# Two units through the first MLP together: the second unit's attention moved beside the first's, its p turned by TensorE in float32

## The chip, the cores and the metric

The kernel runs on one core of a Trainium2 chip. The time is device microseconds from the first to the last instruction, the median of three runs: 1043.31 us before (1042.61 to 1045.53). TensorE (PE, weight loads PEld), VectorE (DVE), ScalarE (ACT), GpSimd (POOL) and the DMA queue of SyncE (SP) work side by side, each in its own fixed order of instructions, and wait for one another by semaphores.

## The reference

Inputs are q, k, v of 4 batches x 8 heads x 576 positions x 64 and a forget gate f (4 x 8 x 576). The weights of both MLPs arrive as float64 bit patterns, which the kernel itself turns into float32.

```python
scores = q @ k.T / 8 + cum[i] - cum[j]     # cum: cumulative sum of log(clip(f)); causal
x  = softmax(scores) @ v                   # 2304 tokens x 512 (8 heads x 64)
h  = x @ w_in                              # first MLP, 512 -> 2048
x1 = (s * relu(h)**2 + b) @ w_out          # 2048 -> 512
h2 = x1 @ w2_in                            # second MLP
out = leaky_relu(h2, 0.01) @ w2_out
```

## The kernel before

**Units.** The 2304 tokens are cut into nine units of 256 tokens. Units 0 to 3 are the first 256 positions of the four batches ("light": a head has 3 blocks of 128x128 scores), units 4 to 7 the next 256 positions and the last 64 ("heavy"), and unit 8 collects the four 64-token tails for the MLP. The first MLP runs unit by unit, 16 steps (`i`) each: `mlp1_h` (L700) makes 128 rows of h for 256 tokens, `mlp1_g` (L714) squares, `mlp1_o` (L740) adds into the output.

**Precision.** A float32 product is made of three passes in the fast float32r form: each operand is split into a high and a low part, and high x high, high x low and low x high are summed. Such a step takes 12 matmuls for h (4 blocks x 3) and 12 for o. The weights are made by `float_w` (L96: one ACT and three DVE instructions on 512 columns) and split by `split_w` (L108: an ACT copy and a POOL subtraction). There are 32 blocks of the first MLP's weights. For unit 0 the w_out blocks are not split: `mlp1_o` uses plain float32 matmuls there (L746, two instructions each in the profile), and the 16 w_out blocks are split during unit 1 (`split_late_to`).

**Attention.** Unit 0 has its own path, done in a startup loop (L622) before the first MLP: `first_a` makes scores, maximum and exponential of a head, `first_b` scales the probabilities p on POOL, turns them by three PE transposes (L597) and copies them out, `first_c` multiplies by v in float32 (L608) and splits the result into `xs[0]`. All other units go by slots, one tile (a head's rows) each, in three stages: `st_score` (L311), `st_split` (L354: p is split into two float16 halves by ACT and DVE and turned by a DMA transpose, L375), `st_av` (L377, AV matmuls L393 on a v that is split and turned in the same way). A pair of heads gathers in `x_raw` and is then split into `xs[u]` (`split_x1`, L426).

**Order.** `slots_to` emits slots beside the MLP steps, as `slot_target` (L668) says: during unit u's MLP the attention of unit u+1. The framework's scheduler then fixes each engine's order ahead of time from these priorities (`ahead`) and from its own estimate of when inputs are ready, so work whose inputs are there fills the gaps, as far as buffers allow: `x` has 2 buffers (units u and u+2 share one), `x_raw` 2, `p_t` and `p_hl` 3, `tt` 4. PSUM's eight banks before: `ps_o` 2 (outputs of two d in one bank), `ps_h` 2, `ps_s` 2, `ps_v` 2.

```python
for u in range(NU):                # L841
    slots_to(ends[u])
    for i in range(NF):            # L851
        ...
        ps = mlp1_h(u, i)
        g = mlp1_g(u, i, ps)
        slots_to(slot_target(u, i))
        if pending is not None: ... mlp1_o(pu, pi, pg, po)
```

Of the kernel before, what the change touches and what calls it, by code (L numbers as in the profile page):

```python
# [17 lines left out]
P = 128  # L18
# [20 lines left out]
def attention_moe_moe_kernel(  # L39
# [31 lines left out]
    wp = ctx.enter_context(tc.tile_pool(name="wp", bufs=2 * NF + 1))  # L71
    ps_o = ctx.enter_context(tc.tile_pool(name="ps_o", bufs=1, space=bass.MemoryType.PSUM))
    ps_h = ctx.enter_context(tc.tile_pool(name="ps_h", bufs=2, space=bass.MemoryType.PSUM))
# [4 lines left out]

    W_FLOAT = 0

# [13 lines left out]
    def float_w(raw, out=None):  # L96
# [7 lines left out]
        out = top if out else x  # L104
        nc.vector.scalar_tensor_tensor(out, low, 29, x, ALU.logical_shift_right, ALU.bitwise_or)  # L105
        return out.bitcast(F32)
# [7 lines left out]
    class Weights:  # L114


        def __init__(self, w_in, w_out, late):
            self.src = (w_in, w_out)
            self.late = late
            self.blocks, self.done, self.split = [], 0, late  # L120
# [4 lines left out]
        def split_to(self, n):  # L125
            while self.done < min(n, len(self.blocks)):
                n0 = self.done
                late = n0 % 2 == 1 and n0 // 2 >= self.late
                x = float_w(self.blocks[n0], late)
                self.blocks[n0] = x if late else split_w(x)  # L130
                self.done += 1

        def split_late_to(self, n):
            while self.split < min(n, NF):
                k = 2 * self.split + 1
                self.blocks[k] = split_w(self.blocks[k])
                self.split += 1
# [4 lines left out]

    w1, w2 = Weights(w_in1, w_out1, W_FLOAT), Weights(w_in2, w_out2, NF)

# [9 lines left out]
    mp = mlp1.enter_context(tc.tile_pool(name="mp", bufs=2, side="right"))  # L154
    att = ExitStack()
# [49 lines left out]
    def load_v(p):  # L205
        if p >= NP:
            return
        u, h = heads[2 * p]
        b, u0, un, _ = units[u]
        kend = u0 + un  # L210
        v_raw[2 * p] = wp.tile([P, 2 * DM], F32, tag="w", name="v_raw")
        nc.sync.dma_start(
            out=v_raw[2 * p][:, :kend], in_=vT[b, h : h + 2, :, :kend].rearrange("h d s -> (h d) s")
        )
# [16 lines left out]
    def split_pair_v(p):  # L231
        if p < NP:
# [121 lines left out]
    def st_split(i):  # L354
# [3 lines left out]
        tt, sm = t_t.pop(i), sm_t.pop(i)  # L358
        nc.vector.tensor_scalar(sm[:, 4 : 4 + nt], sm[:, 2 : 2 + nt], 1.0e-9, 1.0 / PSCALE, ALU.add, ALU.mult)
# [17 lines left out]
    def st_av(i):  # L377
        jb, n, ts, last = tiles[i]
        u, h, j, half = jobs[jb]
        b, u0, un, _ = units[u]  # L380
        if half or (n == 0 and h % 2 == 0):
            av_t[j // 2] = ps_a.tile([P, 512], F32, tag="ps_v", name="ps_v", bufs=2)
# [21 lines left out]
        if not half and h % 2 == 0:  # L404
            x_raw[u] = xp.tile([P, UN + NL], F32, tag="x_raw", name="x_raw", bufs=2)
        xr = x_raw[u]
        at = UN if half else 0
        for e in range(2) if half else [h % 2]:
            own, oth = slice(e * D, (e + 1) * D), slice((1 - e) * D, (2 - e) * D)
            m = NL if half else UN  # L410
            src, o = av[:, e * m : (e + 1) * m], xr[own, at : at + m]
# [4 lines left out]
        if pr == 0:  # L416
            xs[u] = xp.tile([P, 2, ND, UN], F32R, tag="x", name="x", bufs=2)
        inv = v_inv[j - j % 2][:, 4:5]
        with ahead(P_X):
            split_x1(xs[u], pr, xr[:, :UN], inv)  # L420
            if un > UN:
                xl = xr[:, UN:]
                nc.gpsimd.tensor_scalar(xl, xl, inv, 0.0, ALU.mult, ALU.add)
                nc.sync.dma_start(out=xld[pr * P : (pr + 1) * P, b * NL : (b + 1) * NL], in_=xl)

# [4 lines left out]
    def last_x1():  # L430
# [3 lines left out]
        x = xs[NU - 1] = xp.tile([P, 2, ND, UN], F32R, tag="x", name="x", bufs=2)  # L434
# [7 lines left out]
    P_RUN = 4000  # L442

# [6 lines left out]
    W_LATE = 6  # L450
# [38 lines left out]
    for r in range(ND // 2):  # L489
# [3 lines left out]
        if r == 0:  # L493
# [3 lines left out]
            nc.sync.dma_start(out=v_0, in_=v0.rearrange("(k p) c -> p k c", p=P))  # L497
# [4 lines left out]

    cl = wp.tile([P, 2 * DM], F32R, tag="w", name="cum_hl")
# [43 lines left out]
    xs[0] = xp.tile([P, 2, ND, UN], F32R, tag="x", name="x", bufs=2)  # L547
# [416 lines left out]
```

## Time and profile before

| | us |
|---|---|
| median of three runs | 1043.31 |
| profiled execution: its own time / span | 1039.49 / 1037.7 |
| startup, until the first MLP matmul of unit 0 | 0 to 43.6 |
| unit 0's MLP, first output copy | 129.5 |
| unit 1's MLP, first output copy | 191.8 |
| unit 2's MLP, first output copy | 261.4 |
| last output copy of the first MLP on ACT | 639.4 |

In a row of the view by stretches, the first numbers are the stretch and its length, then come each engine's busy time with its count of instructions, the granted TensorE clock as a share of full speed, the share of the DMA engines' time, and the GB/s they moved. In a timeline or chain row stand the start, the duration, and what ran; several like instructions are merged (x12). A matmul's duration includes its way through the array, so a busy PE is not yet a full PE: the distance between starts says how dense it is.

### The profile page before, as it was taken

To read this page: it belongs to the slowest core of one execution; us is meant where nothing else is said; L and a number is where in the kernel's file an instruction comes from. 1 tells how busy PE (TensorE), PEld (TensorE's weight loads), DVE (VectorE), ACT (ScalarE), POOL (GpSimd) and SP (SyncE) were. 2 spreads that over 40 slices of the span, in tenths; PEclk is the share of its full clock that TensorE was granted. 3 is DMA by queue.
4 is the path that set the end of the run, shared out by engine and by line. 5 is a ranking of instruction groups with operands and counts; after the bars stand their busy time and mean duration, and the time that the engine had idled before them with its cause. 6 is when DMAs were issued, how large, how long until landed. Compare 5 with 4: busy or idle time off the path is not lost.

```text
span 1037.7 us, 18127 instructions
## 1 busy us (share of the span) xinstructions
PE 986.1 (95%) x6664; PEld 851.0 (82%) x6664; DVE 537.9 (52%) x1410; ACT 521.3 (50%) x1283; POOL 151.8 (15%) x234
## 2 busy tenths in 40 slices
PE   7887789989999999999999999999999999999998
PEld 4676679879888888888999998778888888888897
DVE  6899773665667766777531399873111311211111
ACT  4777696655656766677643566552221221221232
POOL 4434424110101010100000135430000000000000
PEclk9899999999999999999999999999999999999999
DMA  8499491566889999989620463701000100100010
GB/s 282 152 245 269 89 211 40 136 134 134 186 155 181 180 179 197 185 170 192 90 83 2 168 239 94 239 13 49 33 1 1 61 1 1 41 0 1 1 41 21
DMA packets 184296, 116.68 MB, mean 112 GB/s; under 512 B 137040, under 2 KB 163152, under 8 KB 184208
## 3 DMA queue, kind: packets, MB, share of 16 engines
q1 hardware_dynamic: 184208, 115.53, 47.0%
q8 instruction: 52, 0.85, 0.3%
q14 instruction: 36, 0.29, 0.1%
HBM read 74.00 MB, written 10.04 MB: 81 GB/s over the span
## 4 chain that ended last, share of the span: by engine, by line
PE 47%; issue 3%; DVE 3%; POOL 2%; DMA 1%; ACT 1%; POOLq 0%; SPq 0%; ACTq 0%; DVEq 0%
PE ps_o L823 17%; PE ps_h L807 16%; PE ps_o L749 6%; PE ps_h L705 6%; POOL w L111 2%; PE ps_v L393 1%; DVE wt L103 1%; DMA w_raw<-in_moe_w_out 1%; DVE wt L105 1%; DVE wt L102 1%; PE ps_s L296 1%; DMA p_t<-p_hl 0%; ACT wt L101 0%; PE ps_s L283 0%; DVE g L730 0%
## 5 line engine op out<-in xcount | busy, mean ns | idle before, releaser
L705 PE MATMUL ps_h<-x,w 128*128 128x256 f32 x1728 | 242.9, 286 | 5.0 <-POOL w L111 3.3
L749 PE MATMUL ps_o<-g,w 128*128 128x256 f32 (+1 forms) x1536 | 226.8, 289 | 10.8 <-ACT g L729 6.3
L705 PEld LDWEIGHTS ps_h<-x,w 128*128 128x128 f32 x1728 | 220.4, 190 | 7.7 <-POOL w L111 3.9
L823 PE MATMUL ps_o<-w,g 128*128 128x512 f32 x864 | 216.1, 396 | 1.8 <-DVE g L815 1.8
L807 PE MATMUL ps_h<-x,w 128*128 128x512 f32 (+1 forms) x960 | 213.6, 370 | 0.0
L749 PEld LDWEIGHTS ps_o<-g,w 128*128 128x128 f32 x1536 | 197.3, 190 | 17.5 <-ACT g L729 7.9
L807 PEld LDWEIGHTS ps_h<-x,w 128*128 128x128 f32 x960 | 169.0, 188 | 34.4
L823 PEld LDWEIGHTS ps_o<-w,g 128*128 128x128 f32 x864 | 160.5, 188 | 41.5 <-DVE g L815 3.5
L815 DVE TENSOR_TENSOR g<-ps_h,g 128x512 fp32r<-128x512 f32 (+1 forms) x80 | 51.0, 637 | 258.3 <-ACT g L814 258.1
L813 ACT ACTIVATE ps_h<-ps_h 128x512 f32<-128x512 f32 (+1 forms) x80 | 43.1, 539 | 250.7 <-PE ps_h L807 250.7
L345 ACT ACTIVATE tt<-tt,sm 128x512 f32<-128x512 f32 (+4 forms) x128 | 76.0, 594 | 46.5 <-DVE sm L327 45.2
L371 DVE SCALAR_TENSOR_TENSOR p_hl<-tt,sm,p_hl 128x512 f16<-128x512 f32 (+4 forms) x128 | 77.5, 619 | 34.3 <-ACT p_hl L370 33.8
L370 ACT ACTIVATE p_hl<-tt,sm 128x512 f16<-128x512 f32 (+4 forms) x128 | 73.2, 595 | 40.2 <-DMA p_t<-p_hl 31.6
L111 POOL TENSOR_TENSOR w<-wt,w 128x512 fp32r<-128x512 f32 x48 | 73.6, 1537 | 98.0 <-ACT w L110 92.2
L730 DVE TENSOR_TENSOR g<-ps_h,g 128x256 fp32r<-128x256 f32 x128 | 53.6, 421 | 60.9 <-ACT g L729 59.6
L393 PE MATMUL ps_v<-p_t,v_st 128*128 128x128 f16 (+1 forms) x912 | 59.7, 211 | 14.7 <-DMA p_t<-p_hl 11.9
L727 ACT ACTIVATE ps_h<-ps_h 128x256 f32<-128x256 f32 x128 | 46.8, 367 | 50.3 <-PE ps_h L705 49.4
L393 PEld LDWEIGHTS <-v_st 128*128 128x128 f16 x912 | 44.3, 98 | 21.4 <-issue 13.2
L327 DVE CUSTOM_DVE_ANT_0 tt<-ps_s,cumk 128x512 f32<-128x512 f32 (+4 forms) x128 | 59.6, 497 | 2.2 <-PE ps_s L287 0.7
L101 ACT ACTIVATE wt<-w_raw 128x512 f32<-128x512 f32 x64 | 42.7, 672 | 28.2 <-POOL w L111 19.8
L729 ACT CAST g<-ps_h 128x256 fp32r<-128x256 f32 x128 | 47.2, 370 | 7.9 <-PE ps_o L749 4.4
L728 ACT ACTIVATE ps_h<-ps_h 128x256 f32<-128x256 f32 x128 | 46.9, 368 | 3.0
(91 smaller groups left out, 859.9 us busy)
## 6 DMA issues: line engine op xcount, KB each, us to landing
w_raw<-in_moe_w_in SPq DMA_DIRECT2D x32, 512.0 KB, 5.3
w_raw<-in_moe_w_out SPq DMA_DIRECT2D x32, 512.0 KB, 5.8
cumk<-cumd SPq DMA_DIRECT2D x32, 256.0 KB, 3.9
qk_p<-in_qk SPq DMA_DIRECT2D x16, 480.0 KB, 4.8
x1d<-x1o SPq DMA_DIRECT2D x36, 128.0 KB, 2.9
cumk<-cumd SPq DMA_DIRECT2D x32, 144.0 KB, 3.1
v_raw<-in_v SPq DMA_DIRECT2D x16, 288.0 KB, 3.3
out<-o SPq DMA_DIRECT2D x18, 256.0 KB, 2.3
```

The source lines that it names most:

```text
L111: nc.gpsimd.tensor_tensor(w[:, 1], x, w[:, 0].bitcast(F32), ALU.subtract)
L327: nc.vector.tensor_tensor_reduce(tt[:, at + k0 : at + k0 + kw], ps[:, c, :kw] if half else ps[:, h % 2, at : at + w], cumk[jb][:, k0 : k0 ...
L345: nc.scalar.activation(e, e, AF.Exp, bias=sm[:, r : r + 1], scale=-1.0, accum_out=sm[:, 2 + r : 3 + r])
L370: nc.scalar.mul(v[:, 0, :w], e, inv)
L371: nc.vector.scalar_tensor_tensor(v[:, 1, :w], e, inv, v[:, 0, :w], ALU.mult, ALU.subtract)
L393: nc.tensor.matmul(av[:, at + e * m : at + (e + 1) * m], v_st[j + e][:, k].rearrange("p l d -> p (l d)"), pt[:, to + l * nk + k, e * m : ( ...
L705: nc.tensor.matmul(ps, wi[:, a, d * P : (d + 1) * P], x[:, c, d], start=(d == 0 and n == 0), stop=(d == ND - 1 and n == 2),)
L730: nc.vector.tensor_tensor(out=g[:, 1, :UN], in0=ps, in1=g[:, 0, :UN].bitcast(F32), op=ALU.subtract)
L749: nc.tensor.matmul(po[d], wo[:, a, d * P : (d + 1) * P], g[:, c], start=(first and n == 0), stop=(last and n == 2),)
L807: nc.tensor.matmul(ps[:, :n], wi[:, a, d * P : (d + 1) * P], x[:, e, d, :n], start=(d == 0 and k == 0), stop=(d == ND - 1 and k == 2),)
L815: nc.vector.tensor_tensor(out=g[:, 1, :n], in0=raw, in1=g[:, 0, :n].bitcast(F32), op=ALU.subtract)
L823: nc.tensor.matmul(po[m], g[:, a, m * P : (m + 1) * P], wo[:, e, :], start=(i == 0 and k == 0), stop=(i == NF - 1 and k == 2),)
```

## The change

Units 0 and 1 now go through the first MLP as one, with 512 columns a matmul.

- `x_all` holds the split x of both buffers side by side, so that `mlp1_h` reads 2 x 256 columns. The MLP loop starts at u = 1 with `joint[0]` true; its outputs take four PSUM banks (`ps_o` o0 to o3), and one bank is left for h (`ps_h`, before 2). `mlp1_g` puts relu and square into one SBUF tile `r_all` and splits into g as other units do; the plain float32 o matmuls and `split_late_to` are gone, all 32 blocks are split when they are floated.
- Unit 1's attention is emitted in the startup loop, which has 14 steps instead of 10: from h = 4 on (`U1`) one slot a step. Its scores keep the path of the slots; then p is not split: POOL scales it, `turn` turns it by three float32 PE transposes, `first_av` multiplies with a float32 v (`v_1`, one more load), straight into `xs[1]`. Unit 1's `load_v`, `split_v`, p and v DMA transposes, `x_raw` and `split_x1` are gone.
- The loads of the first q/k pairs and of cum move from steps 6 and 7 to steps 1 and 2. `e_0` uses the buffers of `p_hl`.
- Unit 2's attention runs beside the joint MLP. Its split into `x_all` is held back (`later`, `split_later`) until the joint MLP's steps are emitted, with 3 `x_raw` buffers for its 4 pairs. After the joint MLP, h banks alternate between `ps_h` and o2, AV banks between `ps_v` and o3; `x1o` uses `tt` (joint) or `r_all`.

```diff
-    ps_h = ctx.enter_context(tc.tile_pool(name="ps_h", bufs=2, space=bass.MemoryType.PSUM))
+    ps_h = ctx.enter_context(tc.tile_pool(name="ps_h", bufs=1, space=bass.MemoryType.PSUM))
...
+    x_all = xp.tile([P, 2, 2, ND, UN], F32R, name="x_all")
+    r_all = mp.tile([P, 2, UN], F32, name="r_all", bufs=1)
...
     # st_split
+        if jobs[jb][0] == 1:
+            nc.vector.tensor_scalar(sm[:, 4 : 4 + nt], sm[:, 2 : 2 + nt], 1.0e-9, None, ALU.add)
+            nc.vector.reciprocal(sm[:, 6 : 6 + nt], sm[:, 4 : 4 + nt])
+            p_t[i] = turn(i, tt, {t: (sum(sum(QT[v]) for v in ts[:r]), sm[:, 6 + r : 7 + r]) for r, t in enumerate(ts)})
+            return
...
     # st_av
+        if u == 1:
+            first_av(1, h, p_t.pop(i), ps_a.tile([P, 512], F32, tag="ps_v", name="av_1", bufs=1))
+            return
...
-            x_raw[u] = xp.tile([P, UN + NL], F32, tag="x_raw", name="x_raw", bufs=2)
+            x_raw[u] = xp.tile([P, UN], F32, tag="x_raw", name="x_raw", bufs=3)
...
+        later.append((u, pr, x_raw[u], inv))
+        split_later()
...
+    def split_later():
+        while later and later[0][0] <= read[0] + 2:
+            u, pr, raw, inv = later.pop(0)
+            with ahead(P_X):
+                split_x1(xs[u], pr, raw, inv)
...
+    def turn(n, e, at):
+        for t in at:
+            o = e[:, at[t][0] : at[t][0] + (t + 1) * P]
+            nc.gpsimd.tensor_scalar(o, o, at[t][1], 1.0, ALU.mult, ALU.mult)
+        ps = ps_o.tile([P, 512], F32, tag=f"o{2 + n % 2}", name="ps_t0")
+        pt = ap.tile([P, 5 * P], F32, tag="p_t", name="pt_0", bufs=3)
+        to = 0
+        for k in range(NT0):
+            for t in range(k, NT0):
+                o = at[t][0] + k * P
+                nc.tensor.transpose(ps[:, to : to + P], e[:, o : o + P], ident)
+                to += P
+        nc.scalar.copy(pt[:, :PC], ps[:, :PC])
+        return pt
...
-    for h in range(H + 2):
+    for h in range(U1 + H + LAG):
         with ahead(P_F):
-            if h >= 2:
+            if 2 <= h < H + 2:
                 first_c(h - 2)
...
+        slots_to(h + 1 - U1)
+        if h == 1:
+            load_pair(0)
+            nc.sync.dma_start(out=v_1, in_=v0[1].rearrange("(k p) c -> p k c", p=P))
...
     # slot_target
+        if joint[0]:
+            return ends[1] + ((i + 1) * (ends[2] + LEAD - ends[1])) // NF
...
     # mlp1_h
-                    x[:, c, d],
+                    x_all[:, :, c, d] if joint[0] else x[:, c, d],
...
     # mlp1_g
-        if u == 0 and i >= W_FLOAT:
-
-            g = gp.tile([P, 2 * UN + 4], F32, tag="g", name="g", bufs=2)[:, :UN]
-            nc.scalar.activation(g, ps, AF.Relu)
-            nc.scalar.activation(g, g, AF.Square)
+        if joint[0]:
+            r = r_all.rearrange("p u n -> p (u n)")
+            g = gp.tile([P, 2, 2 * UN], F32R, tag="g", name="g", bufs=2)
+            nc.scalar.activation(r, ps, AF.Relu)
+            nc.scalar.activation(r, r, AF.Square)
+            nc.scalar.copy(g[:, 0], r)
+            nc.vector.tensor_tensor(out=g[:, 1], in0=r, in1=g[:, 0].bitcast(F32), op=ALU.subtract)
             return g
...
     # mlp1_o
-            if u == 0 and i >= W_FLOAT:
-                nc.tensor.matmul(po[d], wo[:, d * P : (d + 1) * P], g, start=first, stop=last)
-                continue
...
-    for u in range(NU):
+    for u in range(1, NU):
...
-            if u == 1:
-                w1.split_late_to(i + W_LATE)
...
+        read[0], joint[0] = u, False
+        split_later()
```

## Rows read from the trace of the kernel before

**Rows 1.** Page, 40 slices of 25.9 us: PE busy tenths and granted clock
```profile
PE   7887789989999999999999999999999999999998
PEclk9899999999999999999999999999999999999999
```

**Rows 2.** Busy time by stretches, all engines, from the startup to unit 2
```profile
8.00:23.50 15.50, 14.71 (x50) 9.64 (x51) 10.82 (x31) 7.75 (x24) 5.99 (x10) 1.00 0.90 313
23.50:37.00 13.50, 11.49 (x62) 8.10 (x63) 11.25 (x31) 8.43 (x26) 6.75 (x8) 1.00 0.73 245
37.00:47.50 10.50, 9.10 (x36) 7.08 (x34) 10.12 (x26) 7.58 (x23) 3.31 (x5) 0.51 0.06 19
...
8.00:43.60 35.60, 31.39 (x127) 21.43 (x128) 28.35 (x73) 21.06 (x61) 16.05 (x22) 0.91 0.67 229
43.60:129.50 85.90, 70.32 (x475) 61.73 (x475) 77.13 (x231) 61.20 (x168) 32.54 (x28) 0.96 0.80 198
129.50:192.00 62.50, 58.33 (x499) 53.68 (x498) 37.70 (x146) 49.72 (x149) 21.30 (x21) 1.00 0.51 119
192.00:263.00 71.00, 65.43 (x564) 59.20 (x563) 44.10 (x131) 40.63 (x104) 7.21 (x21) 0.98 0.66 143
```

**Rows 3.** Timeline of PE: f32 AV matmuls, transposes, and a light pair's scores
```profile
21.74 1.59 PE L608 MATMUL av<-pt,v 128*128 128x256 f32 x4
...
25.57 0.50 PE L597 MATMUL ps_t<-misc,e 128*128 128x128 f32 x3
...
26.81 0.87 PE L608 MATMUL av<-pt,v 128*128 128x256 f32 x4
...
75.25 0.92 PE L296 MATMUL ps_s<-qk_p 64*128 64x256 f32 x8
76.10 0.40 PE L307 MATMUL ps_s<-mask_h,ident_h 128*128 128x128 bf16 x4
```

**Rows 4.** Chain of waits in time order: dozens of matmuls of 256 and 512 columns
```profile
563.17 1.41 PE ps_h L705 x12
564.58 1.45 PE ps_o L749 x12
...
713.15 2.77 PE ps_h L807 x12
715.92 2.80 PE ps_o L823 x12
```

**Rows 5.** Timeline of PE in unit 0: one step's plain float32 matmuls
```profile
57.31 1.89 PE L746 MATMUL ps_o<-g,w_raw 128*128 128x256 f32 x8
```

**Rows 6.** Stretches, only the weights' tile wt: DVE, ACT, POOL
```profile
8.00:43.60 35.60, 17.38 (x25) 9.01 (x14) 5.69 (x4) 0.91 0.67 229
43.60:129.50 85.90, 43.59 (x71) 21.80 (x34) 20.16 (x12) 0.96 0.80 198
```

**Rows 7.** Groups by line and shape, 43.6 to 129.5 us: a light tile's scores on DVE
```profile
L327 DVE CUSTOM_DVE_ANT_0 tt<-ps_s,cumk 128x256 f32<-128x256 f32 x14 | 5.8, 416 | 0.2
...
L327 DVE CUSTOM_DVE_ANT_0 tt<-ps_s,cumk 128x128 f32<-128x128 f32 x14 | 4.0, 282 | 0.0
```

**Rows 8.** Page, groups by line: the 512-column split of g in the second MLP
```profile
L815 DVE TENSOR_TENSOR g<-ps_h,g 128x512 fp32r<-128x512 f32 (+1 forms) x80 | 51.0, 637 | 258.3 <-ACT g L814 258.1
```

**Rows 9.** Stretches, only the score matmuls L296 (8 a light pair)
```profile
43.60:129.50 85.90, 6.23 (x48) 4.63 (x48) 0.96 0.80 198
129.50:192.00 62.50, 6.66 (x48) 4.21 (x48) 1.00 0.51 119
```

**Rows 10.** Stretches, only the AV matmuls L393 (12 a light pair, 48 a heavy)
```profile
200.00:220.00 20.00, 2.04 (x24) 1.35 (x24) 1.00 0.57 127
500.00:520.00 20.00, 4.11 (x74) 3.19 (x74) 1.00 0.50 66
...
43.60:129.50 85.90, 5.18 (x60) 3.69 (x60) 0.96 0.80 198
129.50:192.00 62.50, 3.88 (x48) 2.75 (x48) 1.00 0.51 119
```

More of the change, by code (lines that the diff above doesn't have):

```diff
@@ L114, in attention_moe_moe_kernel, with __init__ @@
     class Weights:
-        def __init__(self, w_in, w_out, late):
+        def __init__(self, w_in, w_out):
             self.src = (w_in, w_out)
-            self.late = late
-            self.blocks, self.done, self.split = [], 0, late
+            self.blocks, self.done = [], 0
         def load(self, eng):
@@ L126, in split_to @@
             while self.done < min(n, len(self.blocks)):
[L127 to L130, printed above, removed]
+                self.blocks[self.done] = split_w(float_w(self.blocks[self.done]))
                 self.done += 1
[L133 to L137, printed above, removed]
         def get(self, i):
@@ L546, in attention_moe_moe_kernel @@
     e_0, sm_0, pt_0 = {}, {}, {}
-    xs[0] = xp.tile([P, 2, ND, UN], F32R, tag="x", name="x", bufs=2)
+    xs.update({u: x_all[:, u % 2] for u in range(NU)})
     def first_a(h):
@@ L620, in first_c @@
         )
-    for h in range(H + 2):
-        with ahead(P_F):
-            if h >= 2:
-                first_c(h - 2)
-            if 1 <= h <= H:
-                first_b(h - 1)
-            if h < H:
-                first_a(h)
-        if h == 3:
-            nc.sync.dma_start(out=sb[:, 0:1], in_=s1.unsqueeze(0).to_broadcast([P, 1]))
-            nc.sync.dma_start(out=sb[:, 1:2], in_=b1.unsqueeze(0).to_broadcast([P, 1]))
-        for _ in range(W_PACE):
-            if len(w1.blocks) < 2 * NF - 5:
-                w1.load(nc.sync)
-        with ahead(P_W):
-            w1.split_to(W_FIRST + W_PACE * h - W_BACK)
-        if h == 6:
-            load_v(0)
-            load_pair(0)
-            load_cumk(0)
-            split_pair_v(0)
-        if h == 7:
-            load_cumk(1)
-            load_cumk(2)
-            load_pair(1)
+    def first_c(h):
+        first_av(0, h, pt_0.pop(h), ps_h.tile([P, 512], F32, tag="h", name="av_0"))
+    joint = [True]
     slot_no = 0
@@ L659, in slots_to @@
             slot_no += 1
+    for h in range(U1 + H + LAG):
+        with ahead(P_F):
+            if 2 <= h < H + 2:
+                first_c(h - 2)
+            if 1 <= h <= H:
+                first_b(h - 1)
+            if h < H:
+                first_a(h)
+        slots_to(h + 1 - U1)
+        if h == 1:
+            load_pair(0)
+            nc.sync.dma_start(out=v_1, in_=v0[1].rearrange("(k p) c -> p k c", p=P))
+        if h == 2:
+            for n in range(NCUM):
+                load_cumk(n)
+            load_pair(1)
+        if h == 5:
+            nc.sync.dma_start(out=sb[:, 0:1], in_=s1.unsqueeze(0).to_broadcast([P, 1]))
+            nc.sync.dma_start(out=sb[:, 1:2], in_=b1.unsqueeze(0).to_broadcast([P, 1]))
+        for _ in range(W_PACE):
+            if len(w1.blocks) < 2 * NF - 5:
+                w1.load(nc.sync)
+        with ahead(P_W):
+            w1.split_to(W_FIRST + W_PACE * h - W_BACK)
     ends = [0]
@@ L742, in mlp1_o @@
         for d in range(ND):
-            first = i == 0 and (u >= UB or d % 2 == 0)
-            last = i == NF - 1 and (u >= UB or d % 2 == 1)
-            if u == 0 and i >= W_FLOAT:
-                nc.tensor.matmul(po[d], wo[:, d * P : (d + 1) * P], g, start=first, stop=last)
-                continue
+            own = u >= UB or u < 2
+            first = i == 0 and (own or d % 2 == 0)
+            last = i == NF - 1 and (own or d % 2 == 1)
             for n, (a, c) in enumerate(((0, 0), (0, 1), (1, 0))):
```

118 lines of the change are left out of this document (61 added, 57 removed).

## The prediction

> **What bounds the kernel now.** I read the page's slices first [rows 1]: from slice 20 on PE is nine tenths busy or more in every slice, at full clock; in the first nine slices it is often at seven or eight, and the clock dips. Since the change touches units 0 and 1, I then went by stretches [rows 2]. From 43.6 to 129.5 us (unit 0's MLP) DVE is busy 77.1 of 85.9 us and PE 70.3. In the second MLP a dozen matmuls follows the last with nothing between [rows 4], so what ends the kernel is PE's backlog: time lost on PE early is lost at the end, and whatever unit 1's end gains, the end gains, if the stages behind it run as before. So I ask when the MLP of units 0 and 1 is done (191.8 us now, its first output copy), and how much of later work PE has done by then.
>
> How full was PE really? Dense dozens of 256 columns start 1.41 (h) and 1.45 us (o) apart, of 512 columns 2.77 and 2.80 [rows 4]. A light pair's scores take 0.85 from the first score to the mask and 0.25 for the mask (0.40 less its way through the array), 1.1 us [rows 3]; an AV matmul is some 0.055 us (48 in 3.88 busy, of which about a third is the way through the array) [rows 10]. In 129.5 to 192 PE had 16 x 2.86 = 45.8 of MLP, 5 light score pairs (5.5), two heavy groups (about 0.9 each) and 2.6 of AV: 55.7 of 62.5 us, a density of 0.89 [rows 4, 9, 10]. In 43.6 to 129.5 it had 16 x (1.41 + 1.5 to 1.9) = 47 to 53 [rows 4, 5] and 10 of attention: 0.66 to 0.73. DVE was the bound there, feeding PE with weights: 43.6 of its 77.1 us went to `wt` [rows 2, 6].
>
> **The change, part by part.**
>
> *Wider matmuls: nothing.* 24 joint matmuls take 5.57 us, two narrow steps 2 x 2.86 = 5.72 [rows 4]. The joint MLP is 16 x 5.57 = 89.1 us; before, units 0 and 1 had 93 to 99. A gain of 4 to 10 us of PE work.
>
> *Unit 1's attention on PE.* It loses 48 float16 AV matmuls (2.6 us) and gains 8 x (0.5 for three transposes + 0.87 for the float32 AV) = 11 us at full clock [rows 3]. So PE's total work is about as before; what can move the end is how the work is packed. DVE loses the p split, the v split and the second x split of unit 1; a head then costs it 0.42 + 0.28 for the scores [rows 7], about 0.35 for small ones and accumulators, and 0.42 for the last subtraction (both estimates, the latter from the same shape): 1.5 us.
>
> *The startup gets longer.* A head of unit 0 costs PE 2.8 us at full clock (23.5 to 37: 11.49 busy for 12 transposes, four heads) [rows 2, 3]. A head of unit 1 costs 0.55 for scores, 0.5 for transposes, 0.87 for AV: 2.0. Eight of each: 38.4 us. At 21.7 us the same AV took 1.59 instead of 0.87 [rows 3], 1.83 times as long: the lower of the two levels, though the row of 8 to 23.5 shows 1.00; I go by the durations. All at the lower level would be 70. So 14.7 busy us up to 23.5 did 8 us worth; the other 30.4 at full clock and the density of 23.5 to 37 (0.85) take 36 us: the joint MLP starts at 59.3. Some low clock will come as it did in 37 to 47.5 (0.51, the 1.2 GHz level) [rows 2]; I take 62. DVE has room: its startup cost was 28.35 us, 17.4 of it for 8 weight blocks [rows 2, 6], so 1.4 a head of unit 0; 8 x 1.4 + 8 x 1.5 = 23 us of attention leave some 26 of 54 us at 0.9 busy, 12 blocks at 2.2. Ends: 54 (full density and clock after 23.5) and 82 (8 + 70 / 0.95, low clock throughout, at the density of 8 to 23.5).
>
> *The joint stage.* PE needs 89.1 + unit 2's attention (4 x (1.1 + 0.66) = 7) = 96 us. 20 weight blocks are left: DVE 44, g 16 x 0.64 = 10 [rows 8], unit 2's attention 22 (77.1 - 43.6 = 33.5 in unit 0's MLP for 14 tiles' scores and 10 heads' AV [rows 2, 6, 7], 2.8 a head): 76 of 105 us, so the weights, two blocks in 6.5 us of PE, keep ahead. The splits of w_out that lay in unit 1's MLP now come here, 16 POOL subtractions of 1.7 (20.16 / 12) [rows 6], beside the other; POOL is at half load. One h bank instead of two costs nothing as long as relu comes within the 2.8 us of the o matmuls between two h; if ACT's queue delays it by 1 us more in each step, 16 us. `r_all`, a single buffer, needs relu to subtraction to end in a step, 2.5 of 5.6 us. Density: 0.89 where attention shared the stage, 1.0 without. I take 0.92: 104.7 us, end at 166.7. Ends: 0.97 (99) and 0.85 (113), which includes the bank.
>
> *The step to unit 2.* Its x may be split only when the last joint h is read, and the fourth pair waits for a free `x_raw`. Four splits and two evictions, about 0.5 us each on ACT and DVE in turn, make some 5 us; two o dozens (5.6 us) cover them, but the second waits for the last g, and o2 for the four output copies. I take 3, ends 0 and 6.
>
> *What is late then.* At 192 PE had issued 8 + 48 + 48 = 104 score instructions (12 light pairs and two heavy groups) and 108 AV (9 pairs) (the first pair's 8 before 43.6) [rows 9, 10]. After the joint MLP the lookahead is cut, since x_raw holds only three pairs: 9 pairs of scores, 8 of AV. That is 3 x 1.1 + 1.8 + 0.7 = 5.8 us of PE work undone, 6.4 at 0.9. So 192 before compares with 185.6.
>
> *Loads, SP.* The early q/k, v_1 and cum loads stand in SP's queue ahead of weight loads. Two pairs (0.25 MB each), v_1 (0.5) and three cum tiles (0.13 each) are 1.4 MB, 4.5 us at the 313 GB/s of 8 to 23.5 us [rows 2], by which weights come later; DVE, busy with heads, hardly wants them then. 16 DMA transposes of unit 1 go. I count 0, ends -2 and +3.
>
> Sum: 185.6 - 166.7 - 3 = 16 us gained. Against the profiled execution: 1039.5 - 16 = 1023.5. The median of the runs stands 3.8 above it; the same 16 off the median gives 1027.
>
> **Rivals.**
>
> *Slower: the startup stays at the low clock.* For it: in 37 to 47.5 the granted clock was 0.51 while PE did transposes and float32 AV with waits, and the change nearly doubles that mixture. Against: 23.5 to 37 ran at 1.00 with 12 transposes among 62 matmuls [rows 2]. At 82 us of startup the joint MLP is over at 187, unit 2's step makes 190: 4 us later than 185.6, 1048. It decides from a startup of about 78 us. The Trainium skill ("TensorE: Matmul & The Clock Gate", Part 4, PE-mode transpose) speaks for it: transposes do not count as PE activity for the clock as other matmuls do. By that rule the startup would go as here, 1048. The trace does not bear it out in 23.5 to 37 and leaves it possible behind.
>
> *Lookahead lost, attention becomes the bound.* Light pairs went at 2 in 20 us when MLP ran beside [rows 10]. Behind the joint MLP five are left, one nearly done: 45 us, so heavy AV begins at 167 + 3 + 45 = 215, where it began at about 222 (108 light ones by 192, 24 in 20 us, 144 in all). It then ran into the stretch of 500 to 520, some 298 us; if that pace is attention's own, the end moves by 7 us only: 1036, and at 12 us a pair not at all. For it: PE was busy only 65.4 of 71 us in 192 to 263 [rows 2]. Against: from slice 10 PE is at nine tenths [rows 1].
>
> *Better packing.* Startup 54, density 0.97, no loss behind: 153, a gain of 32; half way between, 28 us: 1015. For it: two independent chains of heads fill each other's waits. Against: DVE would need its weights done in 45 us.
>
> *It paces on weights after all*, as unit 0 did: 20 blocks at 85.9 / 24 = 3.6 us are 72 us, under 96. Not a case of its own.
>
> **How the numbers follow.** Chances: forecast 0.55 (1016 to 1034 its own range), better packing 0.14, attention bound 0.13, low clock 0.15, the rest 0.03. The outer ends of the terms are 154 (31 gained: 1012) and 82 + 113 + 6 = 201 (15 lost: 1058); the latter needs everything at once, so the range goes from 1011 to 1050. What the runs can't tell from no change is 0.3%, 3 us. Low clock is mostly slower, its better part the same; from the attention case and the forecast's upper end a little the same: faster 0.76, same 0.08, slower 0.16.
>
> **What would show it.** First joint h matmul between 57 and 68 us, with some 12 blocks floated; dozens of joint matmuls 2.8 us apart and steps of 6 to 6.8 us; first joint output copy at 160 to 175; at the step to unit 2 a PE gap under 4 us; heavy AV from about 200; from slice 20 the same digits, shifted. Wrong if the joint steps wait for weights (DVE or POOL ahead of h), if relu comes late to the one bank, if the clock is at 0.5 for over 15 us between 24 us and the joint start, or if a gain at the joint output is gone by 520.

## The result, and the profile after

The changed kernel takes 1060.7 us (median of 4 runs), the kernel before 1044.2 in the same comparison: a ratio of 1.0143, 95% interval 1.0095 to 1.0192. It is 1.4% slower; 1027 was forecast. The profiled executions have spans of 1059.8 and 1037.7 us, 22.1 apart where the medians are 16.5 apart, since the profiled execution before was 4.7 us faster than its kernel's median and the one after 0.9 slower. The experiments turn on three moments in them: the first output copy of the MLP of units 0 and 1 (before 191.8, after 198.1 us), the first relu of unit 2's MLP (189.8, after 209.1), and the end. From the output copy to the end it is 845.9 us before and 861.7 after. So 6.3 us are lost up to the joint output, where 25 had been forecast to be won (191.8 less 166.7), and 15.8 behind it, where 9.4 had been forecast (6.4 of lookahead, 3 for the step).

The page's slices of the kernel after (against [rows 1]): the low ones, which ended with slice 9 before, reach to slice 10.

```profile
PE   5977799798999999999999999999999999999998
PEclk9998889999999999999999999999999999999999
```

The stretches of the kernel after (columns: length, busy us of PE, PEld, DVE, ACT and POOL with their instruction counts, granted clock, DMA share, GB/s), against [rows 2]:

```profile
8.00:23.50 15.50, 10.52 (x39) 6.96 (x38) 12.89 (x33) 7.60 (x20) 8.59 (x14) 1.00 0.98 353
23.50:60.00 36.50, 34.13 (x134) 24.51 (x132) 22.31 (x85) 22.65 (x71) 17.27 (x30) 1.00 0.48 141
...
76.00:146.00 70.00, 56.37 (x257) 41.74 (x257) 68.38 (x147) 52.84 (x124) 30.79 (x20) 0.83 0.70 183
146.00:198.00 52.00, 51.55 (x225) 41.39 (x224) 12.16 (x26) 19.95 (x37) 2.04 (x3) 1.00 0.02 6
198.00:222.00 24.00, 17.76 (x127) 14.23 (x126) 17.62 (x75) 17.00 (x52) 2.01 (x6) 0.79 0.79 194
```

Three things are to be seen. In the startup PE is busy (34.1 of 36.5 us), and yet late. In the joint MLP's first half (76 to 146) DVE is busy 68.4 of 70 us, and PE 56.4 at a clock of 0.83; in its second half PE is full and DVE idle. At the step to unit 2 (198 to 222) PE is busy 17.8 of 24 us at a clock of 0.79.

*Startup.* The AV groups (the four float32 matmuls of a head's p with v) on PE's timeline (start, duration in us; the same operation as in [rows 3]) take the lower level's time until 52 us, where the kernel before had left it at 23.3 and fell back to it only behind 37, though the clock's column shows 1.00 for both:

```profile
38.51 1.62 PE L620 MATMUL av<-pt,v 128*128 128x256 f32 x4
...
48.17 1.60 PE L620 MATMUL av<-pt,v 128*128 128x256 f32 x4
...
56.25 0.82 PE L620 MATMUL av<-pt,v 128*128 128x256 f32 x4
```

The last AV of unit 1 starts at 78.5. The prediction's own marker, the first joint h matmul, comes at 68.1 (57 to 68 forecast), but PE only slips in the matmuls whose heads are ready, and that dozen ends at 87.1. So I take the last AV for the end of the startup.

*Joint MLP.* The weights' tile alone, in the same columns without PE (against [rows 6]): 20 blocks were left at 76 us, and all of their DVE work lies in the first half.

```profile
76.00:146.00 70.00, 43.88 (x59) 23.81 (x39) 30.79 (x20) 0.83 0.70 183
146.00:198.00 52.00, 0.00 (x0) 0.18 (x1) 1.37 (x1) 1.00 0.02 6
```

The joint relus start at 89.9, 97.8, 107.9, ... 149.4, which is 8.5 us a step (59.5 / 7), and from 153.4 on every 5.6. There the dozens follow each other 2.81 us apart (against [rows 4]):

```profile
158.85 2.98 PE L764 MATMUL ps_o<-g,w 128*128 128x512 f32 x12
161.66 2.97 PE L720 MATMUL ps_h<-x_all,w 128*128 128x512 f32 x12
164.47 2.97 PE L764 MATMUL ps_o<-g,w 128*128 128x512 f32 x12
```

*The step to unit 2.* No p was turned between 133.8 and 199.8 us. SP's queue (line, what it waited for, us in total, times, longest) stood at the transposes of v (L248) for 49 us:

```profile
SPq L248 <- DVE g L738: 49.0, 1, 49.0
```

The engine it names had been done; the timeline of DVE shows what it was. The split of v for unit 2's fourth pair (L230 to L243) comes only behind the first x split (L438):

```profile
191.22 0.48 DVE L438 SCALAR_TENSOR_TENSOR x_all<-x_raw,vs,x_all 128x256 fp32r<-128x256 f32 x1 [1.42 <-ACT x_all L437]
191.74 0.42 DVE L230 TENSOR_REDUCE vs<-v_raw 128x1 f32<-128x256 f32 x1
...
194.13 0.48 DVE L243 SCALAR_TENSOR_TENSOR v_hl<-v_raw,vs,v_hl 128x256 f16<-128x256 f32 x1 [0.76 <-POOL v_hl L242]
```

Both use `vs`, the pair's scale, which has three buffers. The changed code holds back unit 2's x splits until the joint h has been read (190.7 us), and each held split still needs its pair's `vs`. With three pairs held, the fourth pair's v can't be scaled, and every transpose and load behind it in SP's queue waits too. Unit 2's fourth x split then comes at 203.4, 11 us behind the third, and its first relu 11.0 us behind the output copy; before, it came 2.0 us ahead of it.

### The profile page after: what moved, and what is told of

Same layout as the page of the kernel before. It is cut to its first block, busy times and chain, and to the rows that moved or that the text cites. A ratio compares the mean times of both kernels' runs of the same rounds, so it can differ in the third digit from the quotient of the medians.

```text
span 1059.8 us, 17356 instructions
## 1 busy us (share of the span) xinstructions
PE 1001.1 (94%) x6352; PEld 847.1 (80%) x6352; DVE 538.0 (51%) x1368; ACT 518.0 (49%) x1237; POOL 149.3 (14%) x242
## 4 chain that ended last, share of the span: by engine, by line
PE 50%; DMA 2%; DVE 2%; issue 1%; POOL 1%; ACT 1%; SPq 0%; POOLq 0%; DVEq 0%; ACTq 0%
PE ps_h L832 18%; PE ps_o L848 18%; PE ps_o L764 6%; PE ps_h L720 6%; DMA x2r<-x1d 1%; PE ps_v L388 1%; POOL w L105 1%; DMA p_t<-p_hl 0%; DVE x L821 0%; DMA x1d<-r_all 0%; PE ps_s L283 0%; DMA w_raw<-in_moe_w_in 0%; DVE wt L98 0%; PE ps_s L270 0%; ACT p_hl L362 0%
## 5 line engine op out<-in xcount | busy, mean ns | idle before, releaser
L764 PE MATMUL ps_o<-g,w 128*128 128x256 f32 (+2 forms) x1536 | 248.2, 304 | 12.7 <-ACT g L746 4.2
L720 PE MATMUL ps_h<-x_all,w 128*128 128x256 f32 (+1 forms) x1536 | 245.0, 304 | 8.4 <-ACT r_all L735 6.3
L720 PEld LDWEIGHTS ps_h<-x_all,w 128*128 128x128 f32 x1536 | 212.0, 193 | 21.1 <-ACT r_all L735 7.4
L832 PEld LDWEIGHTS ps_h<-x,w 128*128 128x128 f32 x960 | 170.0, 189 | 34.6
L105 POOL TENSOR_TENSOR w<-wt,w 128x512 fp32r<-128x512 f32 x64 | 94.8, 1489 | 125.5 <-ACT w L104 118.5
L363 DVE SCALAR_TENSOR_TENSOR p_hl<-tt,sm,p_hl 128x256 f16<-128x256 f32 (+3 forms) x112 | 74.2, 679 | 29.1 <-ACT p_hl L362 28.6
L362 ACT ACTIVATE p_hl<-tt,sm 128x256 f16<-128x256 f32 (+3 forms) x112 | 66.7, 616 | 30.1 <-DMA p_t<-p_hl 17.1
L744 ACT ACTIVATE ps_h<-ps_h 128x256 f32<-128x256 f32 x112 | 41.0, 368 | 53.6 <-PE ps_h L720 53.3
L99 DVE SCALAR_TENSOR_TENSOR wt<-w_raw,wt 128x512 int32<-128x512 int32 x64 | 62.5, 976 | 0.8
L388 PEld LDWEIGHTS <-v_st 128*128 128x128 f16 x864 | 42.5, 99 | 15.8 <-issue 10.1
L104 ACT CAST w<-wt 128x512 fp32r<-128x512 f32 x64 | 39.3, 618 | 30.0 <-DVE wt L99 29.9
```

The costliest lines, as they stand in the source:

```text
L99: nc.vector.scalar_tensor_tensor(x, low, 29, x, ALU.logical_shift_right, ALU.bitwise_or)
L105: nc.gpsimd.tensor_tensor(w[:, 1], x, w[:, 0].bitcast(F32), ALU.subtract)
L362: nc.scalar.mul(v[:, 0, :w], e, inv)
L363: nc.vector.scalar_tensor_tensor(v[:, 1, :w], e, inv, v[:, 0, :w], ALU.mult, ALU.subtract)
L388: nc.tensor.matmul(av[:, at + e * m : at + (e + 1) * m], v_st[j + e][:, k].rearrange("p l d -> p (l d)"), pt[:, to + l * nk + k, e * m : ( ...
L720: nc.tensor.matmul(ps, wi[:, a, d * P : (d + 1) * P], x_all[:, :, c, d] if joint[0] else x[:, c, d], start=(d == 0 and n == 0), stop=(d == ...
```

## The experiments

The theories: A, the startup is what is late, by TensorE's lower level; B, the joint MLP's first half is paced by DVE and ACT, on which weights, unit 2's attention and g are bunched; C and D, unit 2's attention is frozen, by x_raw (C) or by `vs` (D); K, it is the transposes that keep TensorE at the lower level. Ratios are to the kernel before, with 95% intervals; moments are those of the profiled execution ("copy": first joint output copy; "relu": first relu of unit 2). Quoted labels keep the order in which the kernels ran.

**Fillers on PE**

```
 first_a(h):
+    for _ in range(6 if h < 4 else 0):
+        matmul(ps, ident_h, mask_h as 4 x 128, start=True, stop=True)
```

> The kernel after, with six bfloat16 matmuls of 512 columns that nobody reads in front of the scores of each of unit 0's first four heads (24 in all; 24 x 0.21 us = 5 us at 2.4 GHz, 10 at 1.2). Theory A, the startup is long because TensorE stayed at the lower level until 52 us (AV group 1.59 us there, 0.92 behind): if the fillers bring the rise forward to some 30 us, 20 us at half pace become 10; the first AV group of 0.9 us comes near 30 instead of 54, the joint MLP starts near 72 instead of 78 with the fillers paid for, and the time falls by 4 to 8 us, to some 1054. Theory B, the joint MLP's first half is paced by VectorE and ScalarE (weights and unit 2's attention): an earlier start then only meets fewer floated weights, relu of step 8 stays near 153 and the time within 3 us of 1060. If the level doesn't rise earlier, the fillers alone cost 5 to 10 us: 1065 to 1070.

1.0157 (1.0128 to 1.0187), the same as the kernel after. AV groups took 0.9 us at 28 and 32, 1.6 from 37 to 45, 0.9 from 52 on (the last 1.65): the level rose early and fell again, and the last AV came at 78.6. Fillers bought nothing.

**More weights in the startup**

```
-    W_PACE = 1
+    W_PACE = 2
```

> The kernel after, with two weight blocks loaded and floated for each turn of the startup loop instead of one. Theory B (the first eight joint steps take 8.5 us instead of 5.6 because VectorE is 98% busy from 76 to 146, 44 of 68 us of it on weights, while it was idle two fifths of 20 to 60): some 20 blocks are floated by 78 instead of 13, the first eight steps take 6 to 7 us, the last joint relu comes at some 178 to 184 instead of 192.8, and the time falls by 8 to 15 us, to 1045 to 1052. Theory A (it is the clock of the startup): weights don't matter, relu of step 0 near 88 and the time within 3 us of 1060, or later if floats delay the heads. Theory C (the hole at 198 to 222): the joint MLP ends earlier, but unit 2's attention is frozen just the same, and the hole of some 12 us stays.

1.0208 (1.0181 to 1.0234), some 7 us above the kernel after, at intervals that just overlap. The startup itself grew: last AV at 93.5. PE waited for POOL, where the splits of the extra blocks stood in front of the scaling of p (waits of PE, 50 to 100 us):

```profile
PE ps_t L610 <- POOL tt L603: 7.9, 2, 4.6
```

What looked like DVE's idle time in the startup (22.3 busy of 36.5 us) wasn't free for weights.

**A third of the weights' DVE work, in both kernels**

```
-    nc.vector.tensor_scalar(x, x, 3, 0x7FFFFFFF, ...)
-    nc.vector.scalar_tensor_tensor(x, top, -0x80000000, x, ...)
```

> The kernel after without two of the three VectorE passes that turn a weight block from double to single precision (the shift and the sign; the weights are wrong numbers then). This takes 1.4 of 2.2 us of VectorE off each of 64 blocks. Theory B: from 76 to 146 VectorE falls from 68 to 40 us, the first eight joint steps take 6 to 6.5 us, the joint MLP ends 15 us earlier, and the time falls to some 1045. Theory A: the startup still ends near 78, the joint MLP's steps are slow by the clock and not by VectorE, and the time stays within 4 us of 1060.

> The kernel before without the same two VectorE passes of the weights (shift and sign; the weights are wrong numbers). The pair to e3_lite (after: 1060.7 to 1041). Theory B (weights on VectorE pace the joint MLP in the changed kernel more than unit 0's MLP before): before gains less than 12 us (unit 0's MLP, 85.9 us with VectorE 77 busy and PE 70, falls towards 76): 1032 to 1038, and the gap between the kernels narrows to some 5 us. Rival: both are equally paced by weights and the loss lies elsewhere: before gains 18 to 22 us, 1023 to 1026, the gap stays 16 us.

After: 0.9961 (0.9934 to 0.9988), 1.8% or 19 us off the kernel after; before: 0.9929 (0.9901 to 0.9957), 7 us off. After, the copy comes 14.5 us earlier, at 183.6. Before, it comes 6.1 us later (197.9), but that profile's startup was late: its AV groups took 1.5 to 1.65 us until 43.6, and unit 0's first h matmul came at 49.7 instead of 43.6. So stages are to be compared, not moments. First the kernel after without the passes, 76 to 146:

```profile
76.00:146.00 70.00, 63.30 (x300) 48.67 (x297) 43.67 (x99) 52.00 (x121) 25.30 (x18) 0.91 0.56 150
```

then the kernel before without them, unit 0's MLP from its first h to its first copy:

```profile
49.70:130.80 81.10, 73.02 (x510) 64.85 (x509) 58.80 (x189) 64.72 (x182) 28.18 (x29) 0.94 0.85 219
```

DVE has 18 us less to do there than in [rows 2], and the stage is 4.8 us shorter (81.1 against 85.9): unit 0's MLP was bound by DVE much less than I had read by its busy share. The joint stage, from the last AV to the copy, is 13.0 us shorter (106.6 against 119.6). B holds: DVE's load costs the joint MLP more than it cost unit 0's.

**A fourth x_raw, more slots asked for**

```
-  x_raw bufs=3, x_l bufs=2;  ends[2] + LEAD - ends[1]
+  x_raw bufs=4, x_l bufs=1;  ends[2] + 4 - ends[1]
```

> The kernel after with four x_raw buffers instead of three (one x_l instead of two pays for the space), and unit 3's first slots asked for 4 instead of 1 ahead of the joint MLP's end, so that unit 2's fourth pair is evicted and unit 3's scores begin while the joint MLP's second half leaves VectorE and ScalarE idle (146 to 198: VectorE 12 of 52 us busy). Theory C (the step to unit 2 loses some 12 us: PE 17.8 busy of 24 at a clock of 0.79 from 198 to 222): PE is above 21 busy there at full clock, and the time falls by 6 to 10 us, to some 1052. Rival: the attention is only moved, PE's work of it is the same and VectorE's paces it later, and the time stays within 3 us of 1060.

1.0121 (1.0081 to 1.0161): unclear against the kernel after. The tenth turned p still came at 193.4. C falls: x_raw alone wasn't what froze. By the way this profile prices the level: PE begins in the same order as in the kernel after, but its AV groups took 0.9 us from 25 on (1.5 at 39), and the last came at 70.7, not 78.5. It also tells against the clock as what slows the joint MLP's first half:

```profile
76.00:146.00 70.00, 56.53 (x276) 40.88 (x276) 60.84 (x150) 53.66 (x128) 30.42 (x18) 0.96 0.68 172
```

The clock was 0.96 there instead of 0.83, and the first seven steps still took 8.7 us each (81.4 to 142.1).

**Six vs**

```
-  vs bufs=3
+  vs bufs=6
```

> The kernel after with six `vs` buffers instead of three, nothing else. Theory D: what froze unit 2's attention from 134 to 194 us is the pair's scale `vs`, which the held-back x split still needs; with three of them the fourth pair's v split can't start before the first x split (190.7), its transposes leave SP's queue at 194.6, and all later transposes and loads stand behind them. With six, v is split and turned before 150, the transposes of p go on, the wait of 49 us in SP's queue is gone, unit 2's fourth x split comes within 3 us of the third, PE is above 20 busy us of 24 behind the joint output, and the distance from the first joint output copy to the end, 861.7 us, falls to 850 to 856: some 1051 to 1055 in all. Rival (x_raw): the fourth pair needs a fourth x_raw as well, and its x split stays 8 us or more behind the third; gain under 3 us. Rival (order): the scheduler has more to lay beside the joint MLP's first half, which then takes longer by as much.

1.0278 (1.024 to 1.0316): 14 us slower still. At the step all went as D says: relu 2.2 us behind the copy, PE 21.3 busy of 24. But the heavy units got slower, 881.6 us from copy to end. There DVE now takes up v before it is loaded; waits of DVE (300 to 500 us) with six vs:

```profile
DVE vs L230 <- DMA v_raw<-in_v: 19.9, 10, 3.7
```

and in the kernel after:

```profile
DVE vs L230 <- POOL x_l L417: 1.6, 3, 0.7
```

As I read it, three buffers had been the brake that kept this split behind its load in DVE's order.

**Unit 2's attention asked for later**

```
-  ends[1] + ((i + 1) * (ends[2] + LEAD - ends[1])) // NF
+  ends[1] + max(0, i - 7) * (ends[2] + LEAD - ends[1]) * 2 // NF
```

> The kernel after with unit 2's attention slots asked for in the second half of the joint MLP only (behind step 8) instead of evenly over its 16 steps. Theory B: the first half is slow (8.5 us a step) because weights (44 us of VectorE), unit 2's attention and g meet on VectorE and ScalarE there, 68 of 70 us busy, while the second half leaves them idle (12 of 52). Moved, VectorE has some 50 us of work in the first eight steps: they take 6 to 6.8 us, the first joint output copy comes at 183 to 188 instead of 198, and the time falls by 8 to 14 us, less what the attention is later behind it (it froze anyway). Rival: the first half is slow by TensorE's clock alone (0.74 to 0.83 there); the steps stay above 7.5 us with VectorE no longer full. Rival: weights alone pace it, two blocks of 3.5 us each at 7 us a step, whatever else VectorE does: first copy at 194 to 198.

> Both together (unit 2's attention in the joint MLP's second half, six vs buffers) and a fourth x_raw buffer, paid for by one x_l instead of two. If B and D are both right, their gains add: first copy at 183 to 188, 852 to 857 from there to the end: 1037 to 1045, level with the kernel before or just under it. If the attention has no room in the second half (24 us of VectorE in 45 us), unit 2's first relu comes over 12 us behind the first copy again, and the time is that of the better of the two alone.

1.0135 (1.0104 to 1.0167), the same as the kernel after, and with six vs and a fourth x_raw 1.025 (1.021 to 1.0291). The edit hardly moved what it should: DVE was still 66.7 of 70 us busy from 76 to 146, and the first seven joint steps took 8.2 us each. The planner (the framework's scheduler) lays down whatever is ready, so a slot asked for later isn't done much later. These two tell nothing of B. But they show something else: e6's joint steps began 8 us earlier and its copy came at 188.8, 9.3 us before that of the kernel after, and its end only 0.8 us before. From copy to end it took 870.2 us, and e7 877.0.

**Floats held behind g, and the scale held apart**

```
 e9:   with tc.issue_after(g_done[-1].ins):     # behind g of the step before, on DVE
           w1.split_to(18 + i)
 e10:  if joint[0]:
           iv = ap.tile([P, 1], F32, tag="iv", bufs=4)
           nc.gpsimd.tensor_scalar(iv, inv, 1.0, 0.0, ALU.mult, ALU.add)
           inv = iv                             # and x_raw bufs=4, x_l bufs=1
 e12:  both
```

> The kernel after with the joint MLP's weight floats held to a pace on VectorE: each step's floats are queued behind the last subtraction of g, up to block 18 + i at step i (in the kernel after the floats run up to 16 blocks ahead of what PE needs, beside unit 2's attention and in front of g). Theory B: per step VectorE then has some 2.2 (one block) + 0.7 (g) + 1.8 (attention) = 4.7 us, less than PE's 5.6, so all joint steps take 5.6 to 6.5 us; the first joint output copy comes at 175 to 185 (198 in the kernel after) and the time falls by 8 to 15 us, if unit 2's hole behind stays as it is. Rival (clock): the steps up to 146 are slow by TensorE's clock, 0.74 to 0.83; with no waits taken away they stay near 8 us. Rival (floats too late): a step waits for its own block near the end, shown as a wait of PE for POOL's split of w.

> The kernel after with unit 2's scale copied out of vs into a tile of its own (iv, four buffers) and a fourth x_raw (one x_l pays), while vs keeps its three buffers: so the heavy units' order, which six vs buffers spoiled (VectorE waited 20 us there for v_raw), should be that of the kernel after. Theory D: unit 2's fourth x split comes 1 us behind the third, its first relu within 3 us of the first joint copy (11 us in the kernel after), PE busy over 20 of 24 us behind it; of the 8 us gained there some 4 are given back where heavy attention catches up (the eighteenth MLP step behind the joint stage comes 25 us later than before, 19 at the first relu): 1052 to 1057. Rival: the heavy pairs pace from there on, all is given back, within 3 us of 1060.

> Both: paced floats and the copied scale with a fourth x_raw. If B and D are both right: joint steps of 5.6 to 6.5 us, first joint copy at 175 to 185, unit 2's first relu within 3 us of it, and, with what heavy attention takes back, 1040 to 1048. If the heavy pairs pace what comes behind (rival of e10), it is no better than e9 alone.

e10: 1.0007 (0.9983 to 1.0031), the kernel before again: 14 us off the kernel after, by a copy of 128 numbers a pair and a fourth x_raw, which alone (e4) had bought next to nothing. The copy stays at 198.9, the relu comes at 197.5 instead of 209.1, and from copy to end it is 847.3 us, against 845.9 before. The stretch at the step:

```profile
198.00:222.00 24.00, 20.80 (x168) 17.43 (x167) 17.20 (x69) 17.28 (x55) 1.81 (x5) 1.00 0.74 189
```

D is shown, and next to nothing is given back behind it (14 us came back, where I had expected 4 to 8). SP's queue still stands, from 155 on, at the transposes of unit 3's v:

```profile
SPq L248 <- PE ps_v L388: 44.1, 3, 39.8
```

But by then unit 2's four pairs are through: before the copy PE issues 60 AV matmuls (five pairs), in the kernel after 36 (three). e9: 1.008 (1.0052 to 1.0108), 7 us off the kernel after, at intervals that just overlap; copy at 188.3. The floats paused from 92 to 125 us (steps of 5.3 to 6.0 us but for one of 10.2), because their loads were asked for late, and then came two a step (5.0 to 8.1 us). e12: 0.999 (0.9962 to 1.0017), in the median no better than e10, though its profile has copy 187.7 and span 1041.1: 11.2 us earlier than e10 at the copy, 5.1 at the end.

**Unit 1's heads behind unit 0's**

```
-    U1 = 4
+    U1 = 8
```

> The kernel after with U1 = 8 instead of 4: unit 1's heads begin when unit 0's are through, and four more weight blocks are loaded and floated in the startup. Theory A': TensorE rose at 23 us in the kernel before because unit 0's heads alone kept it dense from 9.4 us on, and unit 1's heads among them broke that (10.5 busy of 15.5 us in 8 to 23.5, against 14.7): with U1 = 8 the AV groups fall from 1.6 to 0.9 us near 25 to 30 instead of 52, and some 17 blocks are floated at the joint start; the startup ends by 72 and the time falls by 5 to 8 us. Rival: two chains fill each other's waits, one after the other they leave PE idle; the startup ends at 80 to 88, later than 78.5, and the time is 1060 to 1066.

1.0163 (1.0128 to 1.0198), like the kernel after; last AV at 85.1, with an AV group of 0.87 us at 25 and then 1.4 to 1.7 until 60. The order of the heads doesn't cure the startup. The joint stage was 12 us shorter (107.5 from the last AV to the copy, at 192.6), with four more blocks floated ahead of it, but the end came no earlier than that of the kernel after.

**Even floats; narrow matmuls; transposes as ordinary matmuls** (all on e10)

```
 e13:  as e9, and  while len(w1.blocks) < min(2 * NF, 20 + i): w1.load(nc.sync)
 e14:  for v in range(2): matmul(ps[:, v*UN:(v+1)*UN], w, x_all[:, v, c, d])   # o alike
 e15: -nc.tensor.transpose(ps[:, to:to+P], e[:, o:o+P], ident)
      +nc.tensor.matmul(ps[:, to:to+P], e[:, o:o+P], ident, start=True, stop=True)
 e16:  e13 and e15
```

> e10 (copied scale, fourth x_raw) with the joint MLP's weights loaded and floated evenly, one block a step from 18 + i, in VectorE's queue behind g of the step before. In e12 the floats stopped for five steps (5.6 us each) and then came two a step (6.5 to 7.2 us), because the loads were asked for late. Theory B: with one block a step VectorE has 4.7 us of work in 5.6, all steps come near 5.7 to 6.2, the first joint output copy at 176 to 184 (188 in e12, 199 in e10), and the time falls below e10's by 6 to 12 us: 1034 to 1040, under the kernel before. Rival: the floats' own chain (load, ScalarE, VectorE three times, ScalarE, POOL) delays the blocks of steps 12 to 15, and the time is e12's, 1045. Rival (heavy pairs pace the rest): the joint stage ends earlier and the end doesn't follow.

> e10 with the joint MLP's matmuls done as two of 256 columns each, the same weights twice in a row, instead of one of 512; all else as e10. The term of the prediction (24 joint matmuls 5.57 us against 2 x 2.86 = 5.72): where PE bounds the steps (the second half, 5.62 us a step in the kernel after) a step becomes 5.7 to 5.8 us, in the first half nothing changes; 1 to 2 us in all, within 2 us of e10's 1045.6. Rival: the wide matmuls hide their weight loads better than two narrow ones of the same weights do, a step takes 6.4 us or more there, and the time is 6 us or more above e10.

> e10 with the transposes of the startup (L610, three for each of 16 heads) done as ordinary float32 matmuls against the identity, of the same 128 columns, instead of in transpose mode. Theory K (transposes keep TensorE at the lower level: the AV groups take 1.6 us until 52 us in the kernel after): the AV groups fall to 0.9 us by 30 to 35 and stay there, the last one comes at 66 to 70 instead of 80, and the time falls by 4 to 8 us below e10's 1045.6. Rival (it is the gaps and the small float32 matmuls, whatever their mode): the level rises between 40 and 52 as before, and the time is within 3 us of e10's; if the ordinary matmul takes longer than the transpose, some 48 x 0.1 us more.

> e13 and e15 together. If theory K holds, 4 to 8 us below e13, near 1030; if not, e13's time within 3 us.

e13: 0.998 (0.9956 to 1.0004), about 3 us below e10, at overlapping intervals; copy 193.8. DVE is laid more evenly, but steps are 3.7 to 11.9 us, 6.8 on average. Its stretches:

```profile
76.00:146.00 70.00, 60.18 (x268) 45.68 (x267) 52.48 (x122) 44.22 (x98) 21.38 (x18) 0.87 0.54 137
146.00:198.00 52.00, 51.81 (x266) 41.51 (x265) 32.32 (x78) 33.16 (x73) 11.06 (x12) 1.00 0.37 99
```

So pacing the floats helps as B says, but by 7 us (e9) and 3 (e13) in the medians, where I had expected 8 to 15 and 6 to 12.

e14: 1.001 (0.9988 to 1.0032) against e10's 1.0007, with 5.6 us a step where PE is full: here 512 columns a matmul are worth nothing that can be measured.

e15: 0.9968 (0.9943 to 0.9993), some 4 us below e10, at intervals that just overlap; e16 is as much below e13. So the time came out as K has it, but not its mechanism: in e15's profile the AV groups took 0.87 us at 27 and 30, 1.6 at 37 and 40, 1.5 at 50, and the last came at 80.5 (e10: 80.4; K: 66 to 70). The planner also laid the work out differently, so the 4 us may not be the level's. And the profile shows one of ten executions, at 1043.9 us one of the longer ones (median 1040.6). So K is neither shown nor ruled out. The Trainium skill ("TensorE: Matmul & The Clock Gate", Part 4, PE-mode transpose) says that transpose mode doesn't count as PE-busy in the same way as other matmuls. This trace doesn't bear that out as the only cause of the low spells: e15's startup has no transposes left, and the AV groups still took 1.6 us at 37 and 40.

e16: 0.9929 (0.9907 to 0.9951), 1036.7 us, is the fastest version that does all the work: 0.7% under the kernel before, 2.1% under the kernel after. Copy 186.4, relu 185.0, steps of 5.0 to 9.0 us.

## Why the prediction was wrong

The miss is 38 us in the profiled executions, 16 gained against 22 lost (34 by the medians, 1060.7 against 1027), and three steps make it: startup 16.5, joint stage 14.9, what lies behind 6.4.

*Wider matmuls: right.* A joint step where PE is full takes 5.62 us, forecast 5.57, and in e14 two of 256 cost the same.

*Startup: 62 forecast, 78.5 measured.* Two steps failed. The lower level lasted until 52 us, where I let it end at 23.5. e4's profile, with the level up early, prices that at 8 us. And the density of 0.85, read from 23.5 to 37 before, left some 5 us of idle time, where PE idled 10 us in e4 between 23.5 and 70.7. It waited most for an AV bank, of which each unit has one now (unit 0 had two), until DVE has split x of the head before, and for ACT's copy of the turned p:

```profile
PE av L620 <- DVE x_all L630: 5.6, 6, 1.8
PE av L620 <- ACT pt L612: 2.1, 2, 1.5
```

Another 2.8 us of e4's startup are matmuls of the first joint h, which count to the next stage. What makes the level rise early in one execution and late in another is open. In e1 (fillers), e11 (unit 1's heads behind unit 0's) and e15 (no transposes) it rose by 28 and fell again; but so it did in e12 and e14, whose startup code is that of the kernel after. The floated blocks were right in number (12 by 76 us, 12 forecast), but 14 us late.

*Joint stage: 104.7 forecast, 119.6 measured (78.5 to 198.1).* The failed sentence is "It paces on weights after all ... Not a case of its own". I compared sums, 72 us of weights or 76 of all DVE work under 105 of PE. The sums were nearly right: the 20 blocks took from 76 to 144 us, and DVE was busy 80.5 us from 76 to 198. But they don't lie side by side with PE's: the planner puts every ready float and every ready head first, up to 16 blocks ahead of need, so 68 us of DVE fill the first 70 us while PE goes at 8.5 us a step, and the other eight steps can't go faster than 5.6 to make up for it. PE doesn't wait for weights there; they are early, and relu and the subtraction of g stand behind them and behind unit 2's attention in ACT's and DVE's queues. e3 against e8 shows that this is mostly the changed kernel's own trouble (13 us of the joint stage, 5 of unit 0's MLP); laying the floats out gave 3 to 7 us of it in the medians (e9, e13), and nothing in e12. Behind that point the same half of the MLP is left as behind unit 0's in the kernel before, 45 us of PE, so steps of twice the width didn't move the joint output forward.

*One h bank: right where ACT is free, open elsewhere.* In the second half relu to relu is 5.6 us. In the first half PE waited 6.3 us, in two waits, for relu to read the one bank, and 2.5 for the subtraction of g:

```profile
PE ps_h L720 <- ACT r_all L735: 6.3, 2, 3.5
PE ps_o L764 <- DVE g L738: 2.5, 2, 2.0
```

The work that ACT does in front makes relu late; no run had a second bank, so whether it would have hidden these waits isn't shown.

*The step to unit 2: 3 forecast (0 to 6), 13 measured (from 2.0 ahead of the copy to 11.0 behind it).* I named x_raw as what the fourth pair waits for. It was `vs`, one line away in the same held tuple, and I didn't count who else holds a buffer when a step is held back. This is the loss that turned no change into 1.4% slower: e10 gives it all back.

*Lookahead: 6.4 forecast.* With the freeze cured, 1.4 us are left of the 15.8 behind the joint output (847.3 against 845.9), at a copy that itself comes 7 us later than before. Where the copy comes earlier, more can be left: 853.4 in e12, 849.1 in e16. With e6, e9 and e11, whose gains at the copy hardly or only in part reached the end, this bears on a premise of the prediction: "whatever unit 1's end gains, the end gains, if the stages behind it run as before". They did not run as before. Whether attention paces them then, as the second rival has it, no run settles.

*The rivals.* "The startup stays at the low clock" named half of the startup's loss, and its startup of 82 us was near; its time, 1048, was 13 us short, since I had it alone. With e10, where only startup and joint stage are off, the change is worth nothing, not 16.

## What to carry to other kernels

When a change holds a step back, list every buffer that the held step keeps, the one-column ones too, and follow who allocates the next: in a queue that works in a fixed order one blocked transpose stops all that stand behind it. Compare an engine's work with the stage's length half by half, in the order in which it is issued, not as two sums; and test a "bound" engine by taking work off it, since 18 us less DVE work in unit 0's MLP, where DVE had been busy nine tenths, shortened it by only 5. More buffers can do harm (e5); there, as I read it, their shortage had kept an order in step.

## What the runs showed of the hardware that was not expected

One kernel's own executions differ by 9 to 11 us here (e10: 1042.8 to 1051.5; e16: 1031.4 to 1042.7), and profiles of kernels with the same startup code differ in when TensorE leaves its lower level there (the kernel after 52 us, e4 25). The clock's column shows 1.00 in 23.5 to 60 of the kernel after while the AV groups take 1.6 us until 50, 1.8 times the 0.87 to 0.92 that they take from 55 on; so there I read the level from the duration of one repeated operation, not from the column. A DVE pass over a weight block (L99) takes 0.68 us at the median and 1.78 at the longest, in the stretch where POOL splits weights (76 to 146 us); what lengthens it isn't shown.
